# A new hand-written order of steps for the attention stage and the first MLP units, with 89 small operations on another engine

## The chip, the cores and the metric

The kernel runs on one core of a Trainium2 chip. The metric is the device time of one execution in microseconds (us). It was measured three times for the kernel before; a fourth execution was profiled. Matrix products run on TensorE (PE; its weight loads are listed as PEld), elementwise work on VectorE (DVE), ScalarE (ACT) and GpSimd (POOL), and all large transfers from memory are issued by SyncE (SP).

## What is computed

The reference is block-sparse attention followed by two MLPs. Every query sees its 31 nearest keys and one summary key (the maximum over 32 keys) for each of the 24 blocks of its sequence.

```python
B, H, S, D = 2, 8, 768, 64            # q, k, v
k_sum = k.reshape(B, H, 24, 32, D).max(axis=3)
v_sum = v.reshape(B, H, 24, 32, D).mean(axis=3)
scores_l = q @ k.T / sqrt(D)          # kept where |i - j| < 16, else -1e9
scores_s = q @ k_sum.T / sqrt(D) + log(32)
a = softmax(concat(scores_l, scores_s))
x = a @ concat(v, v_sum)              # 1536 tokens x 512
h = x @ moe_w_in                      # 512 -> 2048
x = relu(h) ** 2 @ moe_w_out          # 2048 -> 512
h = x @ moe2_w_in
g = where(h >= 1, h, where(h <= -1, 0, (h + 1) ** 2 / 4))
out = g @ moe2_w_out
```

Weights come as float64. To keep precision, each matrix operand is held as a high and a low part (`xh`/`xl`, `wih`/`wil`, `woh`/`wol`, `gh`/`gl`), and each product is three matmuls: high by high, high by low, low by high.

## The kernel before

Nothing is looped over in the usual sense. The whole program is one string, `PLAN`, of 2312 words. A word such as `N14v` is the name of a step, its number and, for some steps, the engine that does it (a is ACT, v is DVE, g is POOL). The loop at the end of `build` takes the words one after the other and issues the instructions of each:

```python
for word in PLAN.split():
    name, n, e = re.fullmatch(r"([A-Za-z]+)(\d+)([avg]?)", word).groups()
    step[name](int(n), **({"e": eng[e]} if e else {}))
```

The schedule is manual: each engine executes its instructions, and SP issues its transfers, in the order in which the words put them there. An engine that must wait for an operand holds back everything that the string puts behind that instruction on the same engine. Engines differ only by semaphores between them.

The steps that the text speaks of, with the lines of the kernel before:

- Attention, for 24 groups of 256 queries and two heads: `S` scores (PE, 32 matmuls, L611), `M` mask and maximum (DVE, four custom operations and four short reads, L619), `E` exponential (ACT, four, L625), `Q` row sum (DVE, L628), `R` reciprocal (DVE, L632), `N` normalisation (DVE or POOL, L637), `T` transpose (PE, L642), `to` its copy out of PSUM (L645), `O` product with V (PE, 16 matmuls, L653), `oh` and `ol` the high and low part of the result, tiles `xh` and `xl` (L662 on ACT or DVE, L666 on DVE). `km` is the maximum over key blocks (DVE, L599), `v` and `vk` the block means of V (L679, L688).
- Weights, for each block of 512 KB: `wl` the load (SP, L203, tile `raw`), `dl` and `dq` (ACT, L209, L214), `dr`, `ds`, `dt` (DVE, L216, L218, L220), `da` (POOL, L223), `wh` and `wo` the high and low part (L237, L242), and `sa`, `sh`, `sl` for the sums of weights (L250, L254, L259).
- First MLP units: `H` (PE, L282), `ha`, `hb`, `hh`, `hl` the activation and its two parts (L348 to L377), `Y` (PE, L409), 12 matmuls each.
- From about 110 us on the first layer's product is made in quads `P*` (L314) of a form with fewer products, which needs sums of `x`: steps `u*`, tiles `th`, `tl`, `acc` (L498, L524, L526), 128 by 768 for the first half and 128 by 384 for the second.
- Loads: `kl` keys (L582), `qf`, `ql` queries (L588, L585), `cl` the constants with the mask (L692), `vl`, `bl`, `vf` values.

Of the kernel before, what the change touches and what calls it, by code (L numbers as in the profile page):

```python
# [66 lines left out]
dr4 S8 dl5 dr5 O4 hb0 M8 T6 hh0a oh4a H1 R7 E8 ol4 N7g M9 to6a O5 ds5 hl0g Q8 T7 oh5a ha1a ol5 S10 to7a dt5 dl4 ds4 O6
wl9 da5 M10 E9 Y0 wl6 wl7 oh6v vf2 E10 R8 ol6 N8g Q9 O7 S11 hb1 Q10 R9 dt4 T8 N9g oh7a ql4 hh1a R10 ol7 H3 wl8 to8a
M11 bl2 wh4a kl7 da4 S12 wh5a E11 T9 M12 N10g H2 km6 E12 wo5g S13 Q11 dq6 hl1v O8 wo4g dq7 R11 ha2v Y1 hb2 dr7 ha3a
hh2a M13 dl6 hl2g H5 hb3 to9v N11g hh3a dl7 ds7 S14 E13 hl3g Q12 T10 H4 dr6 oh8a to10a ol8 R12 M14 N12g T11 ha4a Y2  # L70
Q13 to11a km7 E14 v6 ds6 S15 dt7 ha5a hb4 O9 R13 dt6 hh4a ql5 v7 wh7a Q14 Y3 da6 hb5 bl3 oh9v M15 vl4 da7 H6 ol9 R14
hl4v dq9 wh6v v8 hh5v ha6a O10 N14v hb6 v9 dr9 oh10a H7 ol10 uf0v hl5v v10 hh6v O11 ha7v hl6g wo6v v11 hb7 Y4 N13g
vk7a dq8 vk6v vk4v oh11a vk5a ol11 H8 E15 vf4 wo7g vf3 hh7a Q15 T12 dl9 Y6 to12v ha8a dr8 hl7v T13 R15 ds9 Y7 ds8
to13a ua0v hb8 yo7a N15v O12 ub0v S16 oh12a dt8 S17 uc0g ol12 T14 M16 H9 M17 E16 ug0g Y5 dl8 Q16 yo5a wl10 O13 hh8v
da8 R16 ha9v S19 N16v to14a E17 S18 uh0g T15 M18 H10 hb9 oh13a to15a Q17 E18 dt9 hl8g T16 M19 H11 wl11 to16a ol13 hh9a
R17 N17v O14 hl9g Q18 S21 oh14a ha10a da9 R18 ol14 S20 ui0a O15 E19 M20 uj0g T17 vl5 ha11v Y8 E20 M21 N18g oh15a S23
hb10 ol15 to17a uk0v S22 hh10a O16 LW0 wh9v H13 Q20 oh16a wo9g hb11 R20 E21 ul0v N20g Y9 Q19 wh8a ol16 um0a R19 hh11v
saa2g O17 Q21 T18 wo8v un0g oh17a H14 M22 to18a dq11 hl10v E22 H12 hl11g sab2v ud0a N19g Y10 ol17 ha12a dr11 ha14a
hb12 uo0g dq10 Q22 T19 hb14 Y11 M23 to19a hh12a sac2v yo11a T20 dr10 sad2v Pa0 ha13a R21 R22 N21v E23 N22g O18 hl12
H15 oh18a sh4a ol18 up0g Q23 to20a ds11 hh14a O19 sh5a Y12 ha15a sl5g oh19a hl14 hb13 ol19 ds10 O20 sl4g dl11 T21  # L80
oh20v R23 H18 dt10 dl10 dt11 hb15 to21a H16 N23v wl13 da11 hh13a ol20 wl12 wh10a hl13 O21 hh15a wh11a ue0g hl15 T22
oh21v ha16a Y13 ol21 hb16 wo11v uq0a da10 to22a Y14 ur0v dq13 ha18a dl13 O22 T23 wo10v oh22a dq12 H19 ua1g ol22 to23a
dr12 dl12 ub1g dr13 O23 hh16a H17 oh23a ds12 hl16 ol23 ds13 H20 ha17a uc1v dt12 LS0 ud1a dt13 Y15 ue1g wl14 ha20a hb18
wh12v wl15 hb17 ha19a hh17a Pz0 da12 Pc0 hb19 Ca0v yo15a hl17 uf1v Pb0 da13 ug1v dq14 Pd0 hh18a wo12g H21 hl18 dr14
wh13a Cc0a wo13g H22 ds14 saa3g Y16 sab3v ha22a uh1v hb22 ha24a sac3v ha21v Y17 sad3g hh19a hb20 hl19 sh6a dt14 dq15
H23 sl6g sh7a dr15 ui1a Y18 sl7v hb21 ha23a uj1v dl14 Y19 uk1g wl16 hh21v Vb0 yo19a hh20v da14 hl21 Pf0 hl20 ds15 Y20
ul1v ha25v um1a dt15 dl15 un1g Y21 hh22v hb24 wl17 hb25 uo1v Pe0 wh14v up1g hl22 dq16 hh24v hh25a Pa1 da15 hl24 hb23
hh23a Vc0 Y22 uq1a ha26v ur1g hl23 hb26 hl25 wh15a Y23 dr16 ua2g hh26a Ca1v dq17 hl26 Pd1 ub2v ds16 dt16 Pc1 uc2v
ha28v Pb1 Cc1a dr17 ud2a ds17 yo23a Pg0 ue2g Vb1 hb28 Pf1 uf2g ha27a hh28v wh16a dt17 Pe1 wo14g hb27 hl28 wh17a Y24
hh27a Vc1 hl27 ha30a wo15g ug2v dl16 wl18 Y25 dl17 uh2v ha29a wl19 da17 hb30 da16 Pg1 wo17v Pa2 ha31a hh30a hb31 Y26  # L90
hb29 ui2a hh31a uj2g hh29a hl31 Y27 hl29 uk2g hl30 Ca2a saa4g ul2v Pc2 sab4g ya1 um2a ya0 dq19 un2g Pd2 ya3 sh9a wo16v
dq18 Pa3 Cc2a sac4v dr19 Pb2 sad4g ya2 dr18 uo2g Y28 ha32v ds18 hb32 hh32a Vb2 sh8v sl9v Pf2 sl8g up2v Pe2 dl18 Y29
ds19 ha33a dt19 hb33 dt18 uq2a hh33a hl32 ur2g wl20 dl19 Y30 hl33 wh18a Vc2 wl21 da18 Ca3v wh19a ha34v da19 hb34 Y31
wo19g ya5 ya4 Pg2 hh34v wo18g dq21 ya6 hl34 Pd3 ha35v dr21 hb35 Pc3 ds21 dq20 ha36v Pb3 dt21 Cc3a hb36 ya7 hh35a Y32
Vb3 dl21 wh21v dr20 dl20 wl23 da21 hh36a hl36 Pe3 ds20 wo21g hl35 Pf3 Vc3 saa5g dt20 Pg3 ha37a ha38v wh20a wl22 da20
Y33 ha39v hb38 dq23 hb37 wo20g hh38a hb39 Pa4 hh39v sab5v Y34 dq22 hl39 sac5g hh37v sh11a sad5g sl11v sh10a Y35 dr22
sl10g hl37 Ca4v hl38 dl22 Pb4 ya10 dl23 dr23 ya9 Pd4 ds23 ds22 Pa5 ya8 ha40a ya11 dt23 Pc4 dt22 Y36 Cc4a wl24 da22
hb40 wl25 hh40a da23 wh22a hl40 Y37 Vb4 wh23v dq24 wo22v Pe4 wo23g Pf4 Vc4 Pg4 ha41a dq25 Y38 hb41 ha43v dl24 dr25
dr24 hb43 hh41v ha42a ds24 hh43a Y39 hl41 hb42 ds25 hh42a Ca5a hl42 dl25 dt24 Pd5 ya12 wl26 da24 hl43 Pc5 ha44v ya14
Pb5 dt25 Cc5a hb44 wl27 da25 Pa6 hh44a Vb5 wh25a ya13 wh24a Pe5 hl44 wo25g dq26 wo24v saa6g Pf5 Vc5 Pg5 sab6v ha45a  # L100
ya15 dq27 sh13v Y40 sac6v ha47a dr27 hb47 sad6v sl13v ha46v Y41 hh47a hb45 hh45a dl27 hl45 Y42 hb46 dr26 hl47 Ca6a
# [695 lines left out]
```

## Time and profile before

| | us |
|---|---|
| three runs | 588.93, 589.46, 593.23 |
| median | 589.46 |
| profiled execution | 590.83 |
| its span, first to last instruction | 589.0 |
| PE busy | 572.5 (97%) |
| DVE busy | 471.0 (80%) |
| ACT busy | 375.8 (64%) |
| POOL busy | 257.2 (44%) |

The mean granted clock of TensorE was 0.986 of full speed in the profiled execution. The share of busy time is an average: attention and the first units fill most of the first 165 us, quads and the second layer the rest. So the views below are taken by stretch. Borders of the stretches are starts of a step on PE: unit H6 at 66.6 us, O20 at 115.6 us, quad Pg1 at 164.3 us. In a row of such a table there stand the stretch, its length, then busy us (and instructions) of PE, PEld, DVE, ACT and POOL, the granted clock, the share of busy DMA and its GB/s.

### The profile page before, as it was taken

To read this page: it belongs to the slowest core of one execution; us is meant where nothing else is said; L and a number is where in the kernel's file an instruction comes from. 1 tells how busy PE (TensorE), PEld (TensorE's weight loads), DVE (VectorE), ACT (ScalarE), POOL (GpSimd) and SP (SyncE) were. 2 spreads that over 40 slices of the span, in tenths; PEclk is the share of its full clock that TensorE was granted. 3 is DMA by queue.
4 is the path that set the end of the run, shared out by engine and by line. 5 is a ranking of instruction groups with operands and counts; after the bars stand their busy time and mean duration, and the time that the engine had idled before them with its cause. 6 is when DMAs were issued, how large, how long until landed. Compare 5 with 4: busy or idle time off the path is not lost.

```text
span 589.0 us, 11229 instructions
## 1 busy us (share of the span) xinstructions
PE 572.5 (97%) x4272; PEld 531.5 (90%) x4272; DVE 471.0 (80%) x1062; ACT 375.8 (64%) x800; POOL 257.2 (44%) x220
## 2 busy tenths in 40 slices
...
PEclk8888999999999999999999999999999999999999
...
GB/s 336 377 279 288 145 65 92 1 104 76 38 72 75 70 107 83 98 4 118 93 72 30 44 71 2 142 37 108 21 124 0 133 73 51 32 1 1 0 55 160
DMA packets 16529, 54.16 MB, mean 92 GB/s; under 512 B 1724, under 2 KB 2332, under 8 KB 16476
## 3 DMA queue, kind: packets, MB, share of 16 engines
...
q8 instruction: 33, 0.54, 0.4%
...
## 4 chain that ended last, share of the span: by engine, by line
PE 87%; DVE 6%; DMA 4%; ACT 2%; issue 1%; SPq 0%; DVEq 0%; ACTq 0%
PE bank L409 42%; PE bank L314 33%; PE bank L282 5%; DMA raw<-in_wd_dram 3%; PE bank L611 2%; PE bank L653 2%; PE bank L642 1%; PE bank L466 1%; DMA k<-in_kd_dram 1%; DVE s L619 1%; DVE s L637 1%; DVE sm L628 1%; ACT s L625 1%; DVE xl L666 0%; DVE fx L216 0%
## 5 line engine op out<-in xcount | busy, mean ns | idle before, releaser
L223 POOL TENSOR_TENSOR fr<-fx,fr 128x512 uint32<-128x512 uint32 x64 | 85.0, 1338 | 144.6 <-DVE fx L220 95.1
L377 DVE TENSOR_TENSOR gl<-bank,gh 128x384 fp32r<-128x384 f32 (+1 forms) x124 | 65.2, 538 | 16.2 <-ACT gh L373 14.8
L314 PE MATMUL bank<-xh,wih 128*128 128x384 f32 x224 | 75.4, 337 | 0.1
L314 PE MATMUL bank<-xl,wih 128*128 128x384 f32 x224 | 75.1, 335 | 0.0
L409 PE MATMUL bank<-gh,woh 128*128 128x384 f32 (+1 forms) x288 | 66.3, 321 | 0.0
L409 PE MATMUL bank<-gl,woh 128*128 128x384 f32 (+1 forms) x288 | 65.7, 319 | 0.6 <-DVE gl L377 0.6
L409 PE MATMUL bank<-gh,wol 128*128 128x384 f32 (+1 forms) x288 | 65.4, 319 | 0.0
L352 ACT ACTIVATE tm<-bank,bias 128x384 f32<-128x384 f32 x59 | 34.1, 579 | 37.9 <-PE bank L314 25.6
L314 PE MATMUL bank<-xh,wil 128*128 128x384 f32 x224 | 57.1, 335 | 0.0
L314 PE MATMUL bank<-th,wih 128*128 128x384 f32 x168 | 56.7, 337 | 0.1
L314 PE MATMUL bank<-tl,wih 128*128 128x384 f32 x168 | 56.3, 335 | 0.0
L409 PE MATMUL bank<-woh,gh 128*128 128x512 f32 x180 | 55.9, 392 | 0.0
L409 PE MATMUL bank<-wol,gh 128*128 128x512 f32 x180 | 55.9, 391 | 0.0
L409 PE MATMUL bank<-woh,gl 128*128 128x512 f32 x180 | 55.9, 391 | 0.0
L214 ACT ACTIVATE fx<-raw 128x512 f32<-128x512 f32 x64 | 42.5, 668 | 19.6 <-DMA raw<-in_wd_dram 13.4
L369 DVE SCALAR_TENSOR_TENSOR bank<-bank,tm 128x384 f32<-128x384 f32 x64 | 35.5, 560 | 22.4 <-ACT tm L365 15.1
L434 DVE TENSOR_TENSOR acc<-bank,acc 128x384 f32<-128x384 f32 (+1 forms) x81 | 46.7, 601 | 7.3 <-PE bank L409 7.3
L409 PEld LDWEIGHTS bank<-gl,woh 128*128 128x128 f32 x288 | 49.2, 190 | 1.0 <-DVE gl L377 0.9
L373 ACT CAST gh<-bank 128x384 fp32r<-128x384 f32 (+1 forms) x83 | 38.5, 468 | 17.9 <-DVE bank L369 15.3
L409 PEld LDWEIGHTS bank<-gh,woh 128*128 128x128 f32 x288 | 48.9, 189 | 1.0 <-issue 0.4
L409 PEld LDWEIGHTS bank<-gh,wol 128*128 128x128 f32 x288 | 49.4, 191 | 0.0
L209 ACT ACTIVATE fr<-raw 128x512 uint32<-128x512 uint32 x64 | 42.1, 671 | 10.0 <-POOL wil L259 6.5
...
## 6 DMA issues: line engine op xcount, KB each, us to landing
...
```

The lines of the kernel that those rows point to most:

```text
L209: A.activation(fr[n % 2], w_raw(n, 0), AF.Copy, scale=2.0 ** -29)
L214: A.activation(f32(x), f32(hi), AF.Abs)
L223: G.tensor_tensor(fr[n % 2], fx[n % 2], fr[n % 2], ALU.add)
L282: PE.matmul(h_bank(n), a, b, start=i == 0, stop=i == len(ops) - 1)
L314: PE.matmul(q_bank(q, role), a, b, start=bool(first and i == 0), stop=i == 5, skip_group_check=not first)
L352: A.activation(a, h, AF.Relu, bias=bias[:, 1:2], scale=-1.0)
L369: V.scalar_tensor_tensor(h, h, 1.0, a, ALU.max, ALU.mult)
L373: cp(e)(hi, h if m else a)
L377: e.tensor_tensor(lo, h if m else a, f32(hi), ALU.subtract)
L409: PE.matmul(ys[j], a, b, start=f == 0 and i == 0 and (n >= 24 or j % 2 == 0), stop=f == GF - 1 and i == 2 and (n >= 24 or j % 2 == 1))
L434: V.tensor_tensor(a, y_bank(g, t, j), a, ALU.add)
L611: PE.matmul(sbank(i, 2 * h + t)[r * 64:r * 64 + 64, 0 if keys else KW:KW if keys else KN], qs[cc % 2][rows, p, j * QT:(j + 1) * QT], b, st ...
```

## The change

Only the string `PLAN` changes, and its set of 2312 steps stays. The first 750 words stand in another order: all of attention, the decoding of the first weights, the MLP units H0 to H23, the first sums `u*`, the first quads up to Pg1. The last 1562 words are the same as before. Of the reordered steps 89 are on another engine: 28 go from POOL to DVE, 26 from ACT to DVE, 21 from DVE to ACT, 14 from DVE to POOL. The string has one line fewer, so line numbers of the kernel after are lower by one. Its first two lines:

```diff
-warm11 kl0 qf0 cl0 kl1 qf1 kl3 wl1 bl0 km0 kl2 wl0 S0 bl1 M0 wl3 E0 km1 S1 ql1 Q0 vl0 M1 wl2 R0 km3 S3 E1 N0g dq1 Q1
-dl1 T0 dr1 M3 v0 ds1 E3 dt1 v1 km2 v2 wh1a da1 S2 R1 Q3 dl0 N1v wo1g dq0 v3 M2 ql2 v4 kl4 v5 R3 dr0 N3v dq3 T1 ds0 E2
...
+warm11 wl1 kl0 qf0 kl3 kl1 cl0 wl0 qf1 kl2 dl1 ql1 dq1 km0 bl0 dr1 wl3 ds1 S0 km3 wl2 dt1 km1 S1 bl1 da1 vl0 M0 dq0 E0
+M1 S3 dr0 wh1a Q0 E1 ds0 wo1g R0 M3 dl0 S5 km2 N0g E3 Q1 S2 R1 dt0 N1g v0 M2 wh0a v1 v2 Q3 dq3 T1 E2 R3 dr3 N3g T0 M5
...
```

What this does is best seen on single engines. First SP at the start of the program, before: keys, queries and the constants with the mask (`cst`) go first, the first weights (`raw1`) seventh.

```order
L582 DMA k0_112<-in_kd_dram 128x800
L588 DMA q0_110<-in_qd_dram 128x512
L692 DMA cst_109<-in_cd_dram 128x384
L582 DMA k1_113<-in_kd_dram 128x800
L588 DMA q0_110<-in_qd_dram 128x512
L582 DMA k3_115<-in_kd_dram 128x800
L203 DMA raw1_75<-in_wd_dram 128x1024
L698 DMA vw1_136<-in_vb_dram 128x2x1024
```

The same place on SP after:

```order
L202 DMA raw1_75<-in_wd_dram 128x1024
L581 DMA k0_112<-in_kd_dram 128x800
L587 DMA q0_110<-in_qd_dram 128x512
L581 DMA k3_115<-in_kd_dram 128x800
L581 DMA k1_113<-in_kd_dram 128x800
L691 DMA cst_109<-in_cd_dram 128x384
L202 DMA raw0_74<-in_wd_dram 128x1024
L587 DMA q0_110<-in_qd_dram 128x512
```

The load of the first weights now stands ahead of all others, and the constants come sixth in place of third.

Next PE in the middle of attention, before: the end of S13 (keys `k5`), O8 (`pt1` by `acc`), unit Y1 (`gh1`, `gl1` by `woh0`, `wol0`), the first matmul of H5.

```order
L611 MATMUL bank5_68<-k5_117,q1_111 64x96 x2
L611 MATMUL bank6_69<-k5_117,q1_111 64x96 x2
L611 MATMUL bank5_68<-ks5_125,q1_111 64x24 x2
L611 MATMUL bank6_69<-ks5_125,q1_111 64x24 x2
L653 MATMUL bank6_69<-pt1_133,acc_73 64x64 x8
L409 MATMUL bank0_63<-gh1_89,woh0_84 128x256 x2
L409 MATMUL bank1_64<-gh1_89,woh0_84 128x256 x2
L409 MATMUL bank0_63<-gl1_92,woh0_84 128x256 x2
L409 MATMUL bank1_64<-gl1_92,woh0_84 128x256 x2
L409 MATMUL bank0_63<-gh1_89,wol0_86 128x256 x2
L409 MATMUL bank1_64<-gh1_89,wol0_86 128x256 x2
L282 MATMUL bank4_67<-xh_71,wih1_81 128x256
```

The place on PE that holds O8 and Y1 after:

```order
L610 MATMUL bank5_68<-k4_116,q1_111 64x96 x2
L610 MATMUL bank6_69<-k4_116,q1_111 64x96 x2
L610 MATMUL bank5_68<-ks4_124,q1_111 64x24 x2
L610 MATMUL bank6_69<-ks4_124,q1_111 64x24 x2
L652 MATMUL bank6_69<-pt1_133,acc_73 64x64 x8
L408 MATMUL bank0_63<-gh1_89,woh0_84 128x256 x2
L408 MATMUL bank1_64<-gh1_89,woh0_84 128x256 x2
L408 MATMUL bank0_63<-gl1_92,woh0_84 128x256 x2
L408 MATMUL bank1_64<-gl1_92,woh0_84 128x256 x2
L408 MATMUL bank0_63<-gh1_89,wol0_86 128x256 x2
L408 MATMUL bank1_64<-gh1_89,wol0_86 128x256 x2
L281 MATMUL bank4_67<-xh_71,wih1_81 128x256
```

In front of O8 stands S12 (keys `k4`) in place of S13, and behind Y1 stands H4, with S13 behind that; Y1 comes before S13, no longer after it.

Last DVE, around the two `wol2` subtractions (weight blocks 10 and 11) and the sums `u*` of 128 by 768, before: of the low parts `tl0` one is here, and no sum into `acc`, because POOL has those.

```order
L666 TENSOR_TENSOR xl_72<-bank6_69,xh_71 128x256
L377 TENSOR_TENSOR gl1_92<-bank3_66,gh1_89 128x256
L377 TENSOR_TENSOR gl0_91<-bank3_66,gh0_88 128x256
L662 CAST xh_71<-bank6_69 128x256
L666 TENSOR_TENSOR xl_72<-bank6_69,xh_71 128x256
L242 TENSOR_TENSOR wol2_1535<-fr1_79,woh2_1534 128x512
L526 TENSOR_TENSOR tl0_1537<-acc_73,th0_1536 128x768
L242 TENSOR_TENSOR wol2_1535<-fr0_78,woh2_1534 128x512
L666 TENSOR_TENSOR xl_72<-bank6_69,xh_71 128x256
L216 TENSOR_SCALAR fx0_76<-fx0_76 128x512
L216 TENSOR_SCALAR fx1_77<-fx1_77 128x512
```

The place on DVE after that holds the same two `wol2` subtractions:

```order
L525 TENSOR_TENSOR tl0_1544<-acc_73,th0_1543 128x768
L376 TENSOR_TENSOR gl1_92<-bank3_66,gh1_89 128x256
L217 TENSOR_SCALAR fx1_77<-fx1_77 128x512
L219 SCALAR_TENSOR_TENSOR fx1_77<-raw1_75,fx1_77 128x512
L497 TENSOR_TENSOR acc_73<-xh_71,acc_73 128x2x384
L241 TENSOR_TENSOR wol2_1542<-fr0_78,woh2_1541 128x512
L627 TENSOR_REDUCE sm3_140<-s3_131 128x4
L376 TENSOR_TENSOR gl2_93<-bank4_67,gh2_90 128x256
L241 TENSOR_TENSOR wol2_1542<-fr1_79,woh2_1541 128x512
L349 TENSOR_SCALAR bank3_66<-bank3_66 128x256
L497 TENSOR_TENSOR acc_73<-acc_73,xl_72 128x2x384
L525 TENSOR_TENSOR tl0_1544<-acc_73,th0_1543 128x768
```

Two sums into `acc` (L497) and a second low part `tl0` (L525) stand between them now, all 128 by 768 or 2 by 384 wide; they stood on POOL before.

## Rows read from the trace of the kernel before

**Rows 1.** Page: TensorE's clock in 40 slices; packets of DMA queue 8.

```profile
PEclk8888999999999999999999999999999999999999
...
q8 instruction: 33, 0.54, 0.4%
```

**Rows 2.** Busy time of each engine by stretch (columns as told above).

```profile
0.00:7.20 7.20, 5.91 (x51) 2.54 (x51) 1.40 (x9) 1.28 (x1) 0.72 (x9) 1.00 0.75 248
7.20:66.60 59.40, 49.93 (x872) 43.07 (x865) 50.09 (x209) 46.25 (x123) 30.95 (x27) 0.86 0.81 295
66.60:115.60 49.00, 47.08 (x722) 43.50 (x720) 44.25 (x134) 36.05 (x95) 29.47 (x23) 1.00 0.28 82
115.60:164.30 48.70, 48.70 (x401) 47.65 (x402) 43.99 (x78) 34.48 (x77) 33.45 (x27) 1.00 0.21 72
164.30:280.00 115.70, 115.70 (x668) 115.24 (x667) 91.83 (x176) 62.72 (x130) 50.15 (x44) 1.00 0.23 78
```

**Rows 3.** Chain of waits, 0 to 140 us: start, length, what held it.

```profile
51.65 1.44 issue
54.01 2.35 PE bank L409 x12
56.37 2.21 PE bank L282 x12
58.57 0.69 PE bank L611 x32
61.72 1.43 PE bank L409 x12
63.15 0.36 PE bank L679 x8
```

**Rows 4.** Timeline: start, length, instruction, [idle time before it, releaser].

```profile
7.53 1.25 ACT L625 ACTIVATE s<-s,sm 128x120 f32<-128x120 f32 x4 [5.50 <-DVE sm L619]
...
59.73 0.42 DVE L666 TENSOR_TENSOR xl<-bank,xh 128x256 fp32r<-128x256 f32 x1 [3.02 <-ACT xh L662]
```

**Rows 5.** Waits of DVE, 7 to 67 us: total, times, longest.

```profile
DVE s L619 <- PE bank L611: 4.8, 5, 2.2
DVE xl L666 <- ACT xh L662: 3.7, 3, 3.0
```

**Rows 6.** Instructions of DVE by line, 7 to 60 us: busy, mean ns | idle.

```profile
L619 DVE CUSTOM_DVE_ANT_0 s<-bank,cst 128x120 f32<-128x120 f32 x56 | 12.6, 278 | 5.5 <-PE bank L611 4.8 <-PE bank L642 0.3
L628 DVE TENSOR_REDUCE sm<-s 128x4 f32<-128x484 f32 x13 | 8.3, 646 | 1.7 <-ACT s L625 1.7
...
L220 DVE SCALAR_TENSOR_TENSOR fx<-raw,fx 128x512 uint32<-128x512 uint32 x6 | 4.1, 684 | 0.1
L216 DVE TENSOR_SCALAR fx<-fx 128x512 f32<-128x512 f32 x8 | 4.0, 514 | 0.0
...
L218 DVE TENSOR_SCALAR fx<-fx 128x512 uint32<-128x512 uint32 x7 | 3.1, 440 | 0.0
```

**Rows 7.** Instructions of DVE by line, 115.6 to 164.3 us.

```profile
L220 DVE SCALAR_TENSOR_TENSOR fx<-raw,fx 128x512 uint32<-128x512 uint32 x8 | 6.3, 805 | 0.0
L498 DVE TENSOR_TENSOR tm<-tm,xl 128x384 f32<-128x384 f32 x8 | 6.2, 771 | 0.1
L216 DVE TENSOR_SCALAR fx<-fx 128x512 f32<-128x512 f32 x6 | 5.1, 870 | 0.4 <-ACT fx L214 0.4
L218 DVE TENSOR_SCALAR fx<-fx 128x512 uint32<-128x512 uint32 x7 | 4.0, 576 | 0.1
...
L526 DVE TENSOR_TENSOR tl<-acc,th 128x768 fp32r<-128x768 f32 x1 | 2.1, 2052 | 0.0
...
L498 DVE TENSOR_TENSOR tm<-xh 128x384 f32<-128x384 f32 x1 | 0.5, 549 | 0.0
```

**Rows 8.** Sums of 128 by 768 by engine and form, 0 to 175 us.

```profile
L498 DVE TENSOR_TENSOR acc<-acc,xl 128x768 f32<-128x768 f32 x2 | 1.9, 970 | 0.0
...
L498 POOL TENSOR_TENSOR acc<-acc,xl 128x768 f32<-128x768 f32 x4 | 7.7, 1933 | 5.6 <-PE bank L653 5.6
```

More of the change, by code (lines that the diff above doesn't have):

```diff
@@ L67 @@
[L67 to L101, printed above, removed]
@@ new lines @@
+M10 H1 to6a wh2a da2 ol5 M9 dq5 O6 ha1a T7 Q8 dq4 wo2g oh6v H0 hb1 to7a ol6 R8 dr4 dl5 N8v O7 ha0a ds4 S11 hb0 dt4
+hh0a vf2 T8 hh1a dr5 hl0g oh7a E9 kl7 ol7 H3 ds5 hl1v dt5 E10 H2 Q9 wl9 da5 M11 wh5a wl7 Y0 ql4 wh4a km5 bl2 wo5g ha2a
+ha3a hb2 Q10 H5 to8a km4 dl4 hb3 R9 wl8 da4 S12 km6 hh3a vl3 hh2a O8 M12 hl3g Y1 dq6 dr6 oh8a N9v E11 R10 wo4v H4 N10g
+E12 ol8 S13 ha5a hl2g dq7 T9 M13 hb5 Y2 to9a ds6 dr7 O9 Q11 hh5a ha4a S14 ds7 dl6 R11 dt7 N11g T10 km7 wh7a Y3 to10a
+Q12 dl7 dt6 T11 da7 H6 M14 to11a wh6a oh9v da6 hb4 ol9 v6 E14 hh4v v7 S15 bl3 wo6v O10 vl4 R12 v8 hl4v dl8 ql5 N12g
@@ new lines @@
+E21 O16 N18v ul0g S23 R19 Q21 T18 LW0 wh9a H12 M22 E20 wo9v oh16a H13 saa2g E22 ol16 wh8v sab2g Q20 dq10 H14 to18a
+dr10 R21 hb10 N19v sh5a O17 wo8v ha14a sl5g T19 Q22 oh17a hb14 H15 R20 ha12a ol17 hh10a M23 N21g hh11a O18 ha13v hl10g
+sac2v Y9 oh18a to19a ol18 hb12 sad2v ud0a N20v Y10 dq11 hh12v ds10 um0a sh4v O19 dr11 ha15a sl4g hl12 T20 hb15 oh19v
+hb13 R22 Pa0 ol19 to20a dt10 dl10 O20 hl11v wl12 da10 T21 oh20a Y11 ol20 to21a un0v hh13a yo11a hl13 H16 ds11 wh10a
+dt11 dl11 uo0v Y12 wh11a wl13 da11 wo10v E23 H17 N22g ha16a hh14a Q23 dq12 Y13 hl14 wo11v dq13 ha17v O21 up0v hh15a
@@ new lines @@
+dl14 Pa1 uo1v ha25a wl16 da14 hb25 Y20 wl17 hh25v da15 hl21 hl25 Y21 hh23a Ca1v wh14v up1v wh15a Y22 wo14v hb24 uq1a
+hl23 hh24a ur1v Y23 dl16 hl24 ua2g dq17 Vc0 dr17 ha26a Pg0 wo15v hb26 ds17 hh26a Pd1 ub2v dq16 hl26 ha27a Pb1 dr16
+yo23a uc2v ds16 Pc1 hb27 dt16 ud2a dt17 ha28a Y24 da16 Cc1a hh27v dl17 Vb1 hb28 wh17v wl19 da17 hl27 wh16a wl18 Pe1
+hh28a hl28 ue2g Pf1 Vc1 uf2v ha30a Y25 hb30 ug2v uh2v ha29v wo17v Pg1 Pa2 ha31a hh30a hb31 Y26 hb29 ui2a hh31a uj2g
+hh29a hl31 Y27 hl29 uk2g hl30 Ca2a saa4g ul2v Pc2 sab4g ya1 um2a ya0 dq19 un2g Pd2 ya3 sh9a wo16v dq18 Pa3 Cc2a sac4v
@@ new lines @@
+wo47g hc90 hh90a Y86 ha91a hl90 hl89 dt48 hb91 Ca17a Y87 hc91 dl49 wh48v dr49 hh91a dl48 ds49 dt49 Pc17 wh49v wl51
+da49 hl91 wl50 Pb17 Cc17v da48 Pd17 Vb17 ya61 wo49g Pf17 ha92a wo48v Pa18 ya60 hb92 ha93a hc92 Pe17 saa12v sab12v
+hh92a Y88 hb93 hl92 dq51 Vc17 sac12v ha94a hc93 sad12g Pg17 hh93v hb94 hl93 Y89 ha95a Ca18v hc94 sh24v hb95 sl24g
+hh94a hc95 Y90 sh25v dl50 hl94 dq50 dr51 Pc18 sl25v hh95a dr50 ds51 Pb18 Cc18a hl95 ya62 Pd18 dt51 Vb18 Y91 ha96a ds50
+dt50 ya64 hb96 wl52 dl51 hc96 Pf18 wh51a hh96v wl53 da51 hl96 Pe18 ha97a ya66 da50 Pa19 Vc18 wh50a ya65 hb97 wo50g
@@ new lines @@
+Pg18 ha98a hc97 Y92 wo51g dq52 hb98 dr52 dl52 hc98 hh97a Y93 dq53 hl97 dr53 Ca19a ds52 hh98a dl53 hl98 Pd19 ds53 dt53
+Pc19 ha100a wh53v wl55 da53 dt52 Pb19 ha99a wo53g Y94 wl54 hb99 da52 hb100 hc99 hh99a saa13g Cc19a Y95 wh52a Vb19
+sab13g hc100 wo52v hh100a dq55 hl99 Pe19 sac13g ya69 sad13g ya70 Pf19 hl100 Pa20 Vc19 ya68 ha102a Pg19 sh26v sl26v
+ha101a Y96 hb102 hb101 hc102 hc101 Y97 hh102v ha103a sh27v sl27g hb103 dq54 Y98 hc103 dr54 hh103a dr55 hh101a hl103
+ds54 Y99 hl102 ds55 hl101 dt55 Ca20a dl55 ya73 Pc20 dl54 Pb20 Cc20v dt54 Pd20 Vb20 wl56 da54 ya72 wl57 Pf20 ya74 da55
```

137 lines of the change are left out of this document (73 added, 64 removed).

## The prediction

> **What bounds the kernel now.** I read the table of stretches first [rows 2]. From 115.6 us on PE is busy in every microsecond: 48.70 of 48.70 in one stretch, 115.70 of 115.70 in the next. There time is saved only by starting earlier, and since the last 1562 words are the same, what the reordered part gains on PE is handed to the end one for one, as long as PE never runs dry behind it. Before 115.6 us PE has holes: 59.40 less 49.93, or 9.5 us, between 7.2 and 66.6, and 49.00 less 47.08, or 1.9 us, up to 115.6. The granted clock shows a second loss in the same place: 0.86 of full speed from 7.2 to 66.6, and tenths of 8 in the first four of 40 slices [rows 1, 2]; at half speed a matmul takes twice its time while PE counts as busy. Who keeps PE waiting there? DVE is busy 50.09 of 59.40 and ACT 46.25, DMA moves 295 GB/s at a share of 0.81: no engine is full, each waits for the other. DVE's listed waits are 4.8 us for scores from PE and 3.7 for a cast on ACT [rows 5]. The chain of waits [rows 3] has one piece that no operand explains: 1.44 us of "issue" at 51.65, inside S13. Right behind it the clock is low: unit Y1 takes 2.35 us and H5 2.21, where the same 12 matmuls take 1.43 at 61.72. Later DVE stands 3.02 us for the high part of O8, because ACT has that cast behind other work [rows 4].
>
> So the sum has three parts: head (to H6), middle (H6 to O20), and sums (O20 to Pg1). All of it is made against the profiled 590.83 us, which lies 1.4 above the median of 589.46; the last step takes that off.
>
> **The head.** Start first. SP now sends the first weights ahead of keys, queries and mask. The load is 512 KB; at 295 GB/s for a share of 0.81, so 364 at full use [rows 2], it is 0.524 MB / 364 GB/s = 1.4 us by which the first scores are later; and the constants with the mask go from third place to sixth. In return DVE and ACT can decode weights while they wait: ACT idles 5.50 us before its first exponential at 7.53 [rows 4], DVE is busy 1.40 of the first 7.20 [rows 2]. The decoding of one block (0.51 + 0.44 + 0.68 us on DVE [rows 6]) fits in. I set the start at nothing by itself; if the cover fails it costs the 1.4, which the lower end holds.
>
> Next the work that must be done before H6. I counted the steps ahead of H6 in both orders: DVE 95 before and 89 now, ACT 78 and 73, PE 57 and 54, POOL 27 and 25. On DVE two M (12.6/14 = 0.9 us each), two Q (0.65 each) and two R and one N less are about 4 us [rows 6], the other moves (one copy and one ha less, one oh, vk and wo more) cancel. On ACT two E of 1.25 [rows 4], two casts, one keep of V less come to about 3.5. I take the smaller, 3.5. PE postpones S15, v6 and v7: 0.69 + 2 x 0.36 = 1.4 us [rows 3], which must be done later. Net gain of postponing: 3.5 - 1.4 = 2.1.
>
> Then the waits. In the new order Y1 and H4 stand ahead of S13, so between O8 and S13 there is other work, and O8's cast stands ahead of S13's mask. If the stall of 1.44 goes, and with it the low clock behind it, (2.35 - 1.43) + (2.21 - 1.43) = 1.70 is saved too: 3.1 together [rows 3]. Of the 4.8 us that DVE waits for scores [rows 5] I take a quarter, 1.2, as the new order only partly moves work ahead of those waits. Sum of the head: 2.1 + 3.1 + 1.2 = 6.4. Its bounds are 2.1, no wait goes, and 2.1 + 4.8 + 3.7 = 10.6, both of DVE's listed waits go whole [rows 5].
>
> **The middle.** At O20 DVE has done 175 steps in both orders, so the 3.5 us of work put off in the head come back here, while PE has two Y fewer (2 x 1.43 [rows 3]) and its 1.4 back. DVE's idle time there is 49.00 - 44.25 = 4.75 us [rows 2]; PE has 1.5 us less to do in the same stretch, so 4.75 - 1.5 = 3.25 are left for 3.5. It nearly fits. The bounds are 0 and -2.6 (three quarters of the 3.5 show); I take -1.0, because the fit is only on average, and one wait of the kind in [rows 5] is as large.
>
> **The sums.** From O20 to Pg1 DVE gets 20 steps more: five sums of 128 by 768 (0.97 each [rows 8]) are 4.8, seven net of 128 by 384 (0.55 [rows 7]) 3.9, five wo at about 0.68, an uninterrupted decode step's length [rows 6], 3.4, and small ones 1.3: 13.4 us. The room: idle 48.70 - 43.99 = 4.71, and the two Y that PE has more to do, 2.9, make 7.6 [rows 2, 3]. POOL loses as much work as DVE gains (27 steps become 16, 41% less), and DVE is slowed when POOL works beside it: decode steps L216, L218 and L220 take 870, 576 and 805 ns here against 514, 440 and 684 in the head [rows 6, 7], and the sums of 384 wide 771 against 549, one of 768 wide 2052 against 970 [rows 7, 8]. That excess is 6 x 0.356 + 7 x 0.136 + 8 x 0.121 + 8 x 0.222 + 1.08 = 6.9 us; 41% of it, 2.8, should go. 13.4 - 7.6 - 2.8 = 3.0 us do not fit into the stretch. They do fit into the next, where DVE idles 115.70 - 91.83 = 23.9 us [rows 2], if the quads have slack on their operands. So the bounds are -5.8 (no relief at all) and 0; I take -1.0, nearer to 0, because PE was full in this stretch with DVE at 90% [rows 2].
>
> The slowing of DVE beside POOL is in these rows. [...]
>
> **Sum.** 6.4 - 1.0 - 1.0 = 4.4. 590.83 - 4.4 = 586.4 on the profiled execution, 589.46 - 4.4 = 585.1 on the median: I forecast 585.0.
>
> **The rivals.** A measurement of this kernel can tell about 1% from no change, so 583.6 and 595.4 are the borders.
>
> First, DVE takes back what the head gives: the lower ends of middle and an undelayed shortfall, 6.4 - 2.6 - 3.0 = 0.8, so 588.7. For it speaks DVE at 90% in both stretches [rows 2]; against it that PE is not starved there now. Chance 0.20.
>
> Second, the stall stays. If the 1.44 us is PE waiting for its own code, it comes after a count of instructions and not at S13: 4272 matmuls and as many loads over 33 packets of the queue named "instruction" [rows 1] is one packet for some 259 instructions. The same count falls into Y1 in the new order, and stall and low clock come again: 6.4 - 3.1 - 2.0 = 1.3, so 588.2. Chance 0.12. That the wait has no releaser speaks for it; that no other such stall is as long speaks against. [...]
>
> Third, the order fits so well that both listed waits of DVE go: 10.6 - 2.0 = 8.6, so 580.9. For it: the waits are all of cross engine order, which is what changes. Against: the head also depends on loads at a DMA share of 0.81 [rows 2], which no order makes shorter. Chance 0.13.
>
> Fourth, slower: DVE cannot carry the sums. POOL's relief doesn't come, the 5.8 us land on PE as waits for `tl` and `gl` ahead of quads, the middle costs its 2.6 and the head gives only its 2.1: 2.1 - 2.6 - 5.8 = -6.3, so 595.8. It decides from the point where more than the 7.6 us of room plus the later slack is asked of DVE before Pg1. Chance 0.07: it needs all three lower ends.
>
> **Numbers.** The forecast has 0.48. The range 580.5 to 590.5 takes in the third rival's centre, the first and the second; it leaves out the fourth and the tails beyond. Faster by over 1%: the third rival and some of the forecast's upper side, 0.27; slower by over 1%: the fourth, 0.07; within 1%: 0.66.
>
> **What would show it.** H6 starts near 60.2 us in place of 66.6 (64.5 if only postponing counts, 56.0 if all waits go). The mean clock from 7.2 us to H6 is above 0.86, and no "issue" piece of over 1 us stands in the chain around S13 or Y1. From O20 to Pg1 PE is full but for about 1 us in all, with DVE at over 95% and its decode steps nearer to 514 ns than to 870. The distance from H6 to the end grows by about 2 us. The prediction is wrong if H6 is no earlier, through late first scores, or if PE shows waits for DVE between O20 and Pg1 of more than 3 us.

## The result: 589.2 to 582.4 us

The kernel after takes 582.37 us (median of four executions, 581.75 to 582.99), the kernel before 589.19 beside it (four, 588.07 to 593.23): 6.8 us less, a ratio of 0.9872 with a 95% interval of 0.9824 to 0.992. The forecast was 585.0 with 580.5 to 590.5; the time lies inside, 2.6 us below the forecast and 1.5 above the third rival (580.9).

The profiled executions differ by more than the medians: spans of 589.0 and 580.6 us, 8.4 apart. The profiled execution of before took 590.83, 1.6 above its median; what may lie behind that is told below.

TensorE's clock over 40 slices of the kernel after, from its page:

```profile
PEclk8899999999999999999999999999999999999999
```

Two slices are low in place of four [rows 1]. The table of stretches of the kernel after, with borders at M0 (9.9 us), H6, O20, Pg1 (columns as in [rows 2]):

```profile
0.00:9.90 9.90, 5.18 (x51) 2.26 (x51) 4.48 (x14) 2.49 (x3) 1.32 (x10) 1.00 0.82 282
9.90:57.90 48.00, 42.45 (x817) 37.87 (x817) 42.89 (x183) 41.33 (x110) 27.32 (x25) 0.93 0.90 334
57.90:103.00 45.10, 45.10 (x744) 41.68 (x742) 40.88 (x157) 36.73 (x98) 28.12 (x22) 1.00 0.32 98
103.00:155.50 52.50, 51.73 (x427) 50.71 (x427) 48.32 (x97) 35.61 (x81) 19.68 (x16) 1.00 0.24 82
155.50:271.10 115.60, 115.60 (x666) 115.16 (x665) 90.53 (x176) 62.69 (x130) 48.79 (x42) 1.00 0.21 71
```

H6 starts at 57.86 in place of 66.63. From there to O20 PE has no hole (45.10 of 45.10; before 47.08 of 49.00). From O20 to Pg1 DVE does 97 instructions, busy for 48.32 us, in place of 78 in 43.99, and PE misses 0.77 us. The stretch behind, where nothing was reordered, takes the same 115.6 to 115.7.

The chain of waits of the kernel after around S13 answers to [rows 3]; the columns are start, length and what held it:

```profile
47.98 0.61 PE bank L652 x16
48.59 1.62 PE bank L408 x12
50.21 1.44 PE bank L281 x12
51.65 0.69 PE bank L610 x32
```

O8, Y1, H4 and S13 follow each other without a piece of "issue", and S13 takes 0.69 us. DVE's waits from 7 us to H6 answer to [rows 5]:

```profile
DVE s L618 <- PE bank L641: 2.0, 2, 1.6
DVE fx L215 <- ACT fx L213: 1.3, 1, 1.3
DVE xl L665 <- ACT xh L661: 0.8, 2, 0.5
DVE sm L627 <- ACT s L624: 0.4, 1, 0.4
DVE s L618 <- PE bank L610: 0.2, 1, 0.2
```

The mask's waits for scores (L610) fell from 4.8 to 0.2 us, but 2.0 us of its waits now end with a transpose on PE (L641); together they are 2.2. Those for ACT's cast (`xl`) fell from 3.7 to 0.8, so 5.5 of the 8.5 us are gone. A wait of 1.3 us for ACT's `fx` is new. Last the instructions of DVE by line from O20 to Pg1, which answer to [rows 7]:

```profile
L219 DVE SCALAR_TENSOR_TENSOR fx<-raw,fx 128x512 uint32<-128x512 uint32 x7 | 4.7, 683 | 0.1
L217 DVE TENSOR_SCALAR fx<-fx 128x512 uint32<-128x512 uint32 x7 | 4.5, 646 | 0.0
L497 DVE TENSOR_TENSOR tm<-tm,xl 128x384 f32<-128x384 f32 x8 | 4.4, 553 | 0.1
...
L525 DVE TENSOR_TENSOR tl<-acc,th 128x768 fp32r<-128x768 f32 x3 | 2.8, 947 | 0.0
L215 DVE TENSOR_SCALAR fx<-fx 128x512 f32<-128x512 f32 x6 | 2.5, 419 | 0.0
```

The same operations that took 805, 771, 2052 and 870 ns before take 683, 553, 947 and 419; of these five only L217 (576 before) is longer. POOL is busy 19.68 us there in place of 33.45.

To compare kernels whose steps stand in another order I use PE's work done: each PE step counts with its length at full clock (S 0.65, T 0.57, O 0.62, H and Y 1.44, v 0.36, a quad's step 1.05 us), summed in the order in which the steps started in the trace. The lead is how much earlier a kernel has reached the same sum than the profiled execution of before. For before, a sum of 9 is reached at 24.92 us, 15 at 36.80, 27 at 49.37, 36 at 63.08, 66 at 94.15, 132 at 162.26 (Y25, just before Pg1). The leads in us, one profiled execution each:

| kernel | 9 | 15 | 27 | 36 | 66 | 132 |
|---|---|---|---|---|---|---|
| after | -1.8 | 3.4 | 3.7 | 8.2 | 9.2 | 8.9 |
| a_w44 | -1.2 | 3.7 | 3.8 | 8.3 | 9.3 | 9.0 |
| a_pool | -0.9 | 3.0 | 3.3 | 7.5 | 8.0 | 4.7 |
| a_act | -1.7 | 1.0 | 0.8 | 5.2 | 5.5 | 4.0 |
| a_start | -2.8 | 1.6 | 1.7 | 6.2 | 7.2 | 6.9 |
| order_only | -1.8 | 1.0 | 0.8 | 4.5 | -0.9 | -7.6 |
| engines_only | -0.6 | -0.3 | -0.7 | 2.4 | 3.7 | -0.5 |
| before_again | -0.9 | -1.1 | -0.8 | 1.1 | 1.1 | 1.1 |
| b_w44 | -0.1 | -0.2 | -0.2 | 2.7 | 2.7 | 2.6 |
| ba_head | -0.5 | -0.6 | -0.3 | 2.8 | 4.6 | 4.3 |
| ba_start | -2.5 | 1.0 | 1.1 | 5.6 | 6.6 | 6.3 |
| ab_front | -2.5 | 1.1 | -1.3 | 1.3 | 1.2 | 1.1 |
| ab_head | -0.3 | 4.9 | 4.8 | 9.3 | 4.0 | 4.0 |

For the kernel after: it starts 1.8 us behind, wins 5.2 between sums of 9 and 15 (24.9 to 36.8 us of before), 4.5 between 27 and 36 (the stretch of the stall), one more by 66, and keeps it. A lead goes by whole steps of up to 1.44 us, so an entry is good to about 1 us: at a sum of 39, where H6 of the kernel after starts, the lead is 7.2. It is also that of a single execution. Up to a sum of 15 after, a_w44 (but for its warm-up), ab_head and ab_front have the same steps on the same engines, and stand there at 3.4, 3.7, 4.9 and 1.1.

### The profile page after: what moved, and what is told of

It reads as the page before. It is cut to its first block, busy times and chain, and to the rows that moved or that the text cites. A ratio compares the mean times of both kernels' runs of the same rounds, so it can differ in the third digit from the quotient of the medians.

```text
span 580.6 us, 11247 instructions
## 1 busy us (share of the span) xinstructions
PE 565.3 (97%) x4272; PEld 527.3 (91%) x4272; DVE 466.7 (80%) x1081; ACT 373.9 (64%) x795; POOL 237.5 (41%) x206
## 4 chain that ended last, share of the span: by engine, by line
PE 90%; DVE 4%; DMA 4%; ACT 1%; issue 1%; SPq 0%; ACTq 0%; DVEq 0%
PE bank L408 43%; PE bank L313 33%; PE bank L281 6%; DMA raw<-in_wd_dram 3%; PE bank L652 2%; PE bank L610 2%; PE bank L641 2%; PE bank L465 1%; DMA k<-in_kd_dram 1%; DVE fx L215 1%; DVE s L618 1%; DVE sm L627 0%; DVE fx L217 0%; DVE fx L219 0%; PE bank L678 0%
## 5 line engine op out<-in xcount | busy, mean ns | idle before, releaser
L408 PEld LDWEIGHTS bank<-gh,woh 128*128 128x128 f32 x288 | 48.9, 189 | 1.0 <-ACT gh L372 0.4
```

The lines of the kernel that those rows point to most:

```text
L408: PE.matmul(ys[j], a, b, start=f == 0 and i == 0 and (n >= 24 or j % 2 == 0), stop=f == GF - 1 and i == 2 and (n >= 24 or j % 2 == 1))
```

## The experiments

My theory after the result (A): the gain is made in the head in two places, front and stall; the sums on DVE cost nothing because DVE is faster when POOL rests. Rivals were that the stall belongs to single executions, that the order alone gives the gain, that the engines alone give it, and that it comes from the early load of the weights.

**Code counted off elsewhere: b_w44 and a_w44.** The warm-up on PE is cut finer, in the order of before and in that of after; lines of the kernel before:

```diff
-warm11 kl0 qf0 ...
+warm44 kl0 qf0 ...
...
-PE.matmul(bank[4], zero[:, :128], zero, start=True, stop=True)
+PE.matmul(bank[4][:, :128], zero[:, :128], zero[:, :128], start=True, stop=True)
```

Expected of b_w44: 

> The order of before, with the 11 warm-up matmuls of 512 columns at the start of PE cut into 44 of 128 columns: the same columns, but 33 matmuls and 33 loads more ahead of everything else, so that PE's code is counted off 66 instructions earlier. Theory A (the 1.44 us of issue inside S13 are PE waiting for its own code): the stall leaves S13; it goes, or comes about 33 matmuls earlier, and if it goes whole, low clock and all, the time falls by about 3 us, to 586. Rival (the stall belongs to S13, by an operand or a bank that the trace does not name): it stays at S13 with 1.2 to 1.6 us, and the time stays within 1 us of 589.2.

Expected of a_w44: 

> The same cut of the warm-up in the order of after. Theory A (the new order has no protection of its own against the stall, it merely has its code borders elsewhere): one piece of issue of over 1 us may appear in the head, and the time goes up by 1.5 to 3 us, to 584 to 585.5. Rival (the new order itself removes the stall): no such piece, 582.4 within 1 us.

Each run's ratio is to executions of before on the same chip (medians 589.87, 589.23 and 589.4 in the three batches). Measured: b_w44 589.28 us (ten executions, 585.51 to 592.69), ratio 0.9993 [0.9961, 1.0025]; a_w44 582.94 (582.2 to 583.27), ratio 0.9879 [0.9848, 0.9911]. In b_w44's trace the stall in S13 is gone and no other took its place; its lead between 27 and 36 jumps from -0.2 to 2.7. But its median is that of before: the fall to 586 that theory A expected did not come. Its ten executions fall into two groups, five of 585.51 to 588.45 (the profiled one among them) and five of 590.12 to 592.69. So either such a stall and low clock come and go in both kernels, or the shift changed nothing and one execution merely lacked them. a_w44 shows no stall, as after, and its time is within 1 us of after's: that is the rival's forecast.

**The same program again: before_again.** No edit.

Expected: 

> The kernel before itself, for a second profile of the same program. If the 1.44 us of issue inside S13 and the low clock behind it belong to the program, they are there again, at 51 to 58 us. If they belong to single executions, as the profile of before's order up to H6 with after's order behind (no such piece, 2.8 us ahead by 60 us) makes likely, they are gone or elsewhere, and H6 starts 2 to 3 us earlier than at 66.6.

Measured: 589.52 us in one execution. The stall is there again, in the same place of S13; the low clock behind it is not. The chain of waits of before_again:

```profile
51.80 0.61 PE bank L611 x25
52.41 1.04 issue
53.46 0.31 PE bank L611 x7
...
54.38 1.63 PE bank L409 x12
56.01 1.44 PE bank L282 x12
```

Y1 takes 1.63 and H5 1.44 us here, against 2.35 and 2.21 [rows 3]. The same PE order up to H6 ran in two more kernels (ba_head and engines_only, below): neither has the stall. ba_head's chain of waits at the same steps:

```profile
51.30 0.69 PE bank L610 x32
...
52.69 1.63 PE bank L408 x12
54.32 1.44 PE bank L281 x12
```

What differs is the packet of the queue named "instruction" before the stall. The rows of that queue (packets, MB, share of 16 engines) in one microsecond each, first before_again from 50 to 51 us, then ba_head from 48 to 49:

```profile
q8 instruction: 1, 0.02, 9.6%
```

```profile
q8 instruction: 1, 0.02, 6.3%
```

In before and before_again the packet starts at 50.34 us and takes 1.34 and 1.54 us (8.4% and 9.6% of 16 engines for a microsecond); in ba_head and engines_only it starts at 48.83 and 48.38 and takes 1.01 and 0.92. With the late packet PE stands still and goes on some 1.5 us after the packet's end, with the early one it does not stop. That fits a wait for code. It isn't proved: in b_w44 one such packet started 354 matmuls and weight loads of PE after the one ahead of it, 345 in before, and PE did not stop. Why the packet is late stays open.

**Parts of the order: ab_front, ab_head, ba_start, ba_head.** Each takes the first words of one kernel and then all other steps in the order of the other, with the engines of the kernel that a word comes from. The joints, with the last words of the one and the first of the other:

```diff
 ab_front: after  ... E8 ol1 R7 O5   | before ... dt2 da2 dq5 wh2a wo2g H0
 ab_head:  after  ... E14 hh4v v7 S15 | before ... E13 R12 N12g Q13 R13
 ba_start: before ... to1v vk0a da0 S5 | after ... wh0a dr3 M5 dl3 Q2
 ba_head:  before ... M15 vl4 da7 H6 | after  ... hh5a wh6a ol9 wo6v O10
```

Expected of ab_front: 

> The order of after up to O5 (the first 152 words, with after's engines), all that is left in the order of before, with before's engines. Theory A (in equal PE work after is 3.5 us ahead at O5, and nothing before 100 us gives that back): 589.2 - 3.5 = 585.7, and the stall with its low clock may stay or go with the count of PE's instructions; 582.5 to 586. Rival (the gain is in the middle of attention and the first sums, where work went to DVE): 588 to 589.

Expected of ab_head: 

> The order of after up to S15 (the first 290 words, which hold H6), the rest in the order of before with before's engines, so that the sums from O20 on stand on POOL as before. Theory A (the head gives 7 of the 8.9 us, the sums nothing): 589.2 - 5.5 to 7 = 582 to 584. Rival (moving the sums from POOL to DVE is worth several us of its own, as POOL slows DVE): 585 to 587.

Expected of ba_start: 

> The order of before up to S5 (the first 70 words: keys, queries and mask loaded first, the weights later), the rest in the order of after. Theory A (after is 1.8 to 2.2 us behind in equal PE work at its start, because the first weights are loaded and decoded ahead of the first scores): the time falls below after's, 580.5 to 581.5. Rival (decoding the weights early is what frees DVE and ACT for the 5 us gained between 25 and 37 us): 583 to 586.

Expected of ba_head: 

> The order of before up to H6 (the first 297 words), the rest in the order of after with after's engines, sums on DVE too. Theory A (from H6 on the new order saves about 1.8 us of PE waits for xl at 91 to 95 us, and the sums neither cost nor give): 587 to 588. Rival (the 20 more steps on DVE cost PE waits, hidden in after by the lead of its head): 589 to 591; rival (relief from POOL is worth several us): 584 to 586.

Measured: ab_front 590.54 us, ratio 1.0018 [0.9996, 1.0039]; ab_head 589.08, 0.9996 [0.9974, 1.0017]; ba_start 585.07, 0.9928 [0.9893, 0.9963]; ba_head 587.47, 0.9975 [0.9954, 0.9996]. Theory A hits ba_head alone. ab_front and ab_head are slower than either forecast of theirs. ba_start goes to the rival: with before's start and after's rest 2.7 us of after's gain are missing and 4.2 are kept. So the early weights aren't the whole of it; they have a share, if the joint doesn't cost the 2.7. ab_head has the whole lead of after's head (9.3 at 36) and loses 5.3 behind the joint (4.0 at 66): its PE waits 3.0 us in one piece for O behind a mask on DVE, 1.8 more for `xl`, and has a clock of 0.5 from 64.6 to 68.0 us, right behind the long wait. So ab_head doesn't say that the head is worth nothing: here a head of one order and a rest of another don't fit, and the joint costs as much as the head gave. ab_front runs the first 152 words of after, and is 1.1 ahead at 15 where after is 3.4: from 25 to 32 us its clock is at 0.5 of full speed, after's at 1.0, though the steps are the same up to there. One execution of the front says its gain to within 2 us only. Behind its joint ab_front falls from 1.1 to -1.3 at a sum of 27, and by its ten executions after's front ahead of before's rest is worth nothing.

**Engines put back: a_pool and a_act.** The order of after, with the 28 steps that went from POOL to DVE back on POOL (a_pool), or the 47 between ACT and DVE back (a_act). Three words of each:

```diff
 a_pool:
-wo9v  N18v  up0v
+wo9g  N18g  up0g
 a_act:
-to0v  oh0v  to9a
+to0a  oh0a  to9v
```

Expected of a_pool: 

> The order of after with the 28 steps that moved from POOL to DVE put back on POOL, nothing else changed. Theory A (they cost nothing on DVE since decode steps and sums there become shorter, 419 for 870 ns and 553 for 771; on POOL they slow DVE again): L215 and L497 on DVE go back to 700 ns and more in the stretch from O20 to Pg1, and PE waits 1 to 4 us there: 583.5 to 586.5. Rival (which of the two engines holds them does not matter, POOL has room): 582.4 within 1 us.

Expected of a_act: 

> The order of after with the 47 steps that moved between ACT and DVE put back on before's engine, nothing else changed (copies out of PSUM and casts in the front go back to ACT). Theory A (in before the front is held by ACT, which is busy 2.0 of 2 us for 6 us, and some casts on DVE relieve it; the order alone does only part): 584 to 586. Rival (the order alone does it): 582.4 within 1 us.

Measured: a_pool 586.46 us, ratio 0.9957 [0.9933, 0.9981], so 4.1 us worse than after, as theory A has it. (The 14 steps that went from DVE to POOL stay there, so POOL has more to do than in before: 41.85 us against 33.45 in the row below and [rows 2].) Its instructions of DVE by line, and its row of stretches, both from O20 (104.4) to Pg1 (159.7):

```profile
L219 DVE SCALAR_TENSOR_TENSOR fx<-raw,fx 128x512 uint32<-128x512 uint32 x8 | 7.9, 1001 | 0.1
...
L217 DVE TENSOR_SCALAR fx<-fx 128x512 uint32<-128x512 uint32 x7 | 5.9, 839 | 0.1
L497 DVE TENSOR_TENSOR tm<-tm,xl 128x384 f32<-128x384 f32 x7 | 4.9, 704 | 1.7 <-POOL tm L497 1.6
L215 DVE TENSOR_SCALAR fx<-fx 128x512 f32<-128x512 f32 x6 | 3.3, 554 | 0.5 <-ACT fx L213 0.5
```

```profile
104.40:159.70 55.30, 52.84 (x427) 50.68 (x427) 47.01 (x79) 35.81 (x81) 41.85 (x32) 1.00 0.22 77
```

DVE has 18 instructions fewer than in after and is busy only 1.3 us less, since each takes longer (683 to 1001, 646 to 839, 553 to 704, 419 to 554 ns) while POOL works 41.85 us in place of 19.68. L215 stays short of the 700 ns that was expected. PE idles 2.5 us in place of 0.8. Its lead falls from 8.0 at 66 to 4.7 at 132, while after's falls by 0.3.

a_act is 586.08 us, ratio 0.9946 [0.9929, 0.9963], 3.7 worse than after. In its trace the loss is in the front: 1.0 ahead at 15 where after is 3.4, as order_only (1.0), which has the same engines there but for three normalisations. The rows of stretches from a sum of 9 to one of 15, for before, after, a_act and ab_front:

```profile
24.90:36.80 11.90, 9.10 (x123) 7.46 (x124) 9.74 (x30) 11.39 (x31) 7.97 (x7) 0.79 0.91 318
26.70:33.40 6.70, 6.58 (x175) 5.56 (x176) 6.25 (x30) 6.00 (x17) 4.68 (x5) 1.00 0.79 245
26.60:35.90 9.30, 8.00 (x177) 6.66 (x180) 6.51 (x29) 8.05 (x24) 5.35 (x5) 0.84 0.96 324
27.40:35.70 8.30, 8.30 (x175) 7.24 (x176) 6.02 (x28) 6.24 (x17) 4.42 (x5) 0.73 0.87 274
```

With copies and casts on DVE (after), DVE is busy 6.25 of 6.70 us and PE has next to no holes, 0.1 us; with them on ACT (a_act), DVE is busy 6.51 of 9.30 us and PE idles 1.3. In before ACT is busy 11.39 of 11.90 us and PE idles 2.8. But the clock differs too: 1.00 in after, 0.84 in a_act, and 0.73 in ab_front, which has after's engines, no holes, and yet takes 8.30 us. So of the 2.6 us that a_act takes longer than after here, 1.3 are holes and 1.4 are time that PE is busy longer, at the lower clock. What is the engines' doing, and what the single execution's, one trace each doesn't part; the 3.7 us on the medians are from ten executions.

**Order alone and engines alone: order_only and engines_only.** The order of after with before's engine in all 89 words, and the order of before with after's; two of the words each.

```diff
 order_only: (order of after)
-to0v ... wo9v
+to0a ... wo9g
 engines_only: (order of before)
-to0a ... wo9g
+to0v ... wo9v
```

Expected of order_only: 

> The order of after with all 89 moved steps back on before's engine: the order alone. Undoing the 28 moves from POOL to DVE cost 4.1 us and undoing the 47 between ACT and DVE cost 3.7 us. Theory B (order and engines are one fit, each move serves a place in this order, and most of the gain goes when the engines don't fit the order): 588 to 591, near the 589.2 of before. Rival (order and engines are worth something each, and the losses add): 582.4 + 4.1 + 3.7 = 590.2 at most, or 586 to 588 where the two losses cover each other.

Expected of engines_only: 

> The order of before with the 89 steps on after's engines: the engines alone. Theory B (a fit of both): no gain, 589 to 593, since DVE gets 20 steps more from O20 to Pg1 without the places cleared for them. Rival (DVE works faster when POOL rests, in any order): 584 to 587.

Measured: order_only 596.63 us, ratio 1.0122 [1.0075, 1.0169]; engines_only 592.13, ratio 1.0041 [1.0018, 1.0064]. Both are slower than before, and together they are 6.8 us faster. The four corners: before 589.4, engines alone +2.7, order alone +7.2, both -6.8 (beside its own executions of before). If the two were independent, both would be near 599. engines_only is within the forecast of theory B; order_only is slower than either of its forecasts.

order_only loses 5.4 us between 36 and 66, and 6.7 more by 132. Its profiled execution took 599.47, 2.8 more than the other three (596.55 to 596.63), so these losses are larger than the median has them. The largest single loss is at 79 to 87 us. The rows of stretches there, and what DVE and PE do on their timelines (start, length, instruction, [idle time before it, releaser]):

```profile
79.00:82.00 3.00, 2.70 (x38) 2.42 (x32) 3.00 (x2) 2.12 (x4) 3.00 (x3) 1.00 0.58 182
83.90:87.30 3.40, 3.38 (x39) 3.33 (x39) 1.68 (x10) 1.23 (x5) 0.00 (x0) 0.50 0.14 40
```

```profile
78.38 3.86 DVE L636 TENSOR_TENSOR s<-s,sm 128x480 f32<-128x480 f32 x2
...
89.31 0.65 DVE L636 TENSOR_TENSOR s<-s,sm 128x480 f32<-128x480 f32 x1
```

```profile
83.51 0.83 PE L610 MATMUL bank<-k,q 64*64 64x96 f32 x6 [1.81 <-DVE sm L618]
```

Two normalisations of 128 by 480 hold DVE for 3.86 us, 1.9 each where one takes 0.65 at 89.31 with POOL at rest; POOL works all 3.0 us of the first row beside them. The mask behind them comes late, PE waits 1.81 us for it, and behind that its clock is at 0.5 for 3.4 us. Then POOL itself is late; its timeline:

```profile
91.65 1.85 POOL L376 TENSOR_TENSOR gl<-tm,gh 128x256 fp32r<-128x256 f32 x2 [8.29 <-ACT gh L372]
93.46 1.83 POOL L497 TENSOR_TENSOR acc<-acc,xl 128x768 f32<-128x768 f32 x1
95.37 1.83 POOL L525 TENSOR_TENSOR xl<-acc,xh 128x768 fp32r<-128x768 f32 x1
```

POOL waits 8.29 us for a cast on ACT, and the 768-wide sums stand behind that wait on its queue; from them the chain of waits goes on over DVE to an O at 99.34, for which PE idles 0.92. From O20 to Pg1 PE is busy 53.28 of 57.00:

```profile
114.90:171.90 57.00, 53.28 (x425) 50.63 (x426) 48.38 (x80) 36.53 (x83) 38.32 (x31) 1.00 0.22 75
```

engines_only holds its lead to 66 (3.7) and loses 4.2 by 132, where DVE has the sums but the order has no place for them; PE waits there for DVE 1.3 us at a quad and 1.2 at `xl` (waits of PE from H6 to Pg1):

```profile
PE bank L314 <- DVE bank L327: 1.3, 1, 1.3
PE bank L653 <- DVE xl L666: 1.2, 3, 0.5
```

**The start: a_start.** In the order of after the first scores come ahead of the first weights:

```diff
-warm11 wl1 kl0 qf0 kl3 kl1 cl0 wl0 qf1 kl2 dl1 ql1 dq1 km0 bl0 dr1 wl3 ds1 S0 km3 wl2 dt1 km1 S1 bl1 da1 vl0 M0 dq0 E0
+warm11 kl0 qf0 cl0 wl1 kl3 kl1 wl0 qf1 kl2 dl1 ql1 dq1 km0 bl0 S0 M0 dr1 wl3 ds1 km3 wl2 dt1 km1 S1 bl1 da1 vl0 dq0 E0
```

Expected: 

> The order of after with its start changed: keys, queries and mask are loaded ahead of the first weights, and M0 stands ahead of the decoding of those weights on DVE (30 words at the beginning, the same steps and engines). Theory A (after is 1.8 to 2.2 us behind at its start in equal PE work, and that is given to the end): 580.5 to 581.5. Rival (the loss at the start is made good before 30 us anyway, because decoded weights are what the front then needs; or the start decides the rest of the front): 582.4 to 585.

Measured: 584.46 us, ratio 0.9912 [0.9883, 0.9942], 2.1 worse than after. Theory A falls here, and the rival (582.4 to 585) holds. M0 is 3.4 us earlier, but what comes next is later; PE's timeline at the second scores:

```profile
9.97 0.60 PE L610 MATMUL bank<-k,q 64*64 64x96 f32 x8 [3.59 <-DMA k<-in_kd_dram]
12.49 0.42 PE L610 MATMUL bank<-ks,q 64*64 64x24 f32 x8 [1.93 <-DVE ks L598]
```

The keys of the second scores now come behind the weights, and PE waits 3.59 us for them and 1.93 for their block maximum on DVE. DMA has little room in this stretch (from 3 to 14 us a share of 0.94 here, 1.01 in after), so what is put first delays something else; at a sum of 9 a_start is 2.8 behind, after 1.8.

## Why the forecast held, and where its steps did not

**The start** was set at nothing, with 1.4 as its cost if the cover fails. It fails: M0 starts at 9.9 in place of 7.2, and after is 1.8 behind at 9 (with the same words a_w44 is 1.2, ab_front 2.5 and ab_head 0.3 behind, so about 1 in the mean against before's own executions, of which the four others in the table are 0.1 to 0.9 behind). But the start seems to pay later: a kernel with before's start (ba_start) is 2.7 slower than after, one with the loads turned round (a_start) 2.1. So the term had the wrong size at its place, and had nothing for what the early weights may give behind it.

**Work postponed, 2.1.** H6 is 8.8 us earlier, of which 7.2 is a lead in equal work (sum of 39) and about 1.5 is work moved behind it, the 1.4 of S15, v6 and v7. My 2.1 counted the relief of DVE and ACT as if it were time of PE; what DVE and ACT save is in the leads of the next point.

**Stall and low clock, 3.1.** The step that failed: "If the stall of 1.44 goes, and with it the low clock behind it [...] 1.70 is saved too", as a gain of the new order. The size is right: ba_head, with before's head and without the stall, is 3.1 ahead between 27 and 36. But it does not belong to before's order as such. Of five profiled executions with before's order of PE up to H6 two have the stall, and one the low clock behind it. So the whole 3.1 could not be counted against the median of before. Two profiled executions of after's full order and engines (after and a_w44) have no such stall, and their eight times lie within 1.6 us of each other, so a part of the 3.1 may count: how often either kernel stalls stays open. The stall may be what puts the profiled execution of before 1.6 above its median; that is not shown, for before_again has a stall of 1.04 us and lies at the median (589.52 against 589.4).

**Waits, 1.2.** Between 9 and 15 after wins 5.2 us, four times that. This is the front, in two halves. In the rows from a sum of 9 to one of 15 PE idles 2.8 us in before and 0.1 in after. What PE waited for there in before is named by its own waits, from 24.9 to 36.8 us; in after none is listed:

```profile
PE bank L282 <- DVE xl L666: 1.0, 2, 0.7
PE bank L653 <- ACT pt L645: 0.9, 1, 0.9
PE bank L282 <- ACT xh L662: 0.8, 1, 0.8
```

These are copies and casts that go by ACT, or stand behind one. With ACT's casts back on ACT 2.7 of the 5.2 are won (a_act). Of DVE's listed waits 5.5 of 8.5 us went; the third rival had all of them go, and the measured time is nearer to it than to the forecast. The other 2.5 are time that PE was busy longer in before, at a clock of 0.79 against 1.00: after has none of the low stretches that before has at about 24 to 27 and 34 to 37.5 us. The rows of stretches for 24 to 34 us have a granted clock of 0.84 in before, 0.51 in before_again and 0.50 in ba_head, against 1.00 in after and 0.83 in a_act. ab_front has such a stretch in after's order, and wins 3.6 in place of 5.2 with it, so the order doesn't exclude it.

**The middle, -1.0.** PE has 1.5 us less to do there, and the stretch became 3.8 shorter (48.9 to 45.1): a gain of 2.3. I had DVE's put-off steps fill the room. The 1.9 us of PE's holes in this stretch stand in my text on what bounds the kernel, but my sum has no term for them; 1.8 of them are waits of O14 and O15 for `xl` from DVE (before, 66.6 to 115.6 us):

```profile
PE bank L653 <- DVE xl L666: 1.8, 2, 1.0
```

In after there are none.

**The sums, -1.0.** PE has 2.9 more to do and the stretch is 3.7 longer: -0.8. The first rival (DVE takes it back) and the fourth (slower) are wrong. The relief was larger than I took: of the 6.9 us by which POOL slowed DVE, 1.4 are left (7 x 0.206 for L217 against 440 ns), so 80% went and not 41%.

The slowing is a matter of POOL being at work beside DVE, and a_pool shows it by giving POOL its work back: with POOL busy 41.85 us in place of 19.68, sums of two tiles (L497) take 704 ns on DVE in place of 553, and L215, which has one input, 554 in place of 419. In what way POOL slows DVE, no run shows. a_pool takes 28 steps off the fuller DVE, and is 4.1 us slower than after. The -5.8 of my lower bound, no relief at all, did not come.

**The sum.** In the profiled executions: head 7.2, middle 2.3 and sums -0.8 make 8.7 (8.9 by the lead at 132, the pieces are rounded); 0.5 is lost behind that, so 8.4 at the end. On the medians it is 6.8, since the profiled execution of before lies 1.6 above its median. That the time came within the range is partly luck: postponed work that is no lead (2.1) and a stall that counts in some executions only (3.1) stood in for a front that was too small (1.2) and a middle with the wrong sign (-1.0).

The second rival (the stall comes back by code) was wrong for after. Of what should show the steps, H6 at 60.2 came at 57.9, no issue piece of over 1 us is there, the clock rose from 0.86 to 0.93, PE missed 0.8 between O20 and Pg1; DVE is at 92% there, not over 95. From H6 to the end it is 522.8 us in place of 522.4: 0.4 more, not 2.
